# One decode step on a Trainium2 core: a load of sixteen rows of 64 bytes put ahead of the first weight load on SyncE's queue

## The chip, the cores and the metric

The kernel runs on one core of one Trainium2 chip. The metric is device time in microseconds (us) of one execution; lower is better. The kernel before was timed three times: 186.65, 186.67 and 186.84 us, median 186.67 us. Durations of single steps come from one more execution that the hardware profiler recorded. Its own time is 186.95 us, and its span, from the first to the last recorded instruction, is 185.7 us.

## The reference

One decode step of a transformer block for a batch of two tokens of width 640, all in bf16: attention over a cached window, then a gated feed-forward network, both modulated by a condition vector `c`.

```python
mod = (_silu(c) @ w_mod).reshape(2, 6, 1, 640)      # sa, ca, ga, sb, cb, gb
h = _layernorm(x) * (1 + ca) + sa
q = (h @ wq).reshape(B, Sq, 32, 192)                # 32 heads of 192
k, v = k_cache[:, :, Sk - W:], v_cache[:, :, Sk - W:]   # W = 1024 of 4096 rows
p = _softmax(einsum(q, k) * 192 ** -0.5)
x = x + ga * (einsum(p, v) @ wo)
h = _layernorm(x) * (1 + cb) + sb
x = x + gb * ((_gelu(h @ w_gate) * (h @ w_up)) @ w_down)
```

Every weight and every row of the cached window is used once, so each has to be brought in from HBM once: the page counts 76.88 MB read.

## The kernel before, in words

The big loads are all issued by SyncE (SP), one after the other, in the order in which the program lists them, through the helper at L252 (`e.dma_start`). All of them therefore show as "SPq L252" in the profile. That order is: `w_mod` (4800 KB, into place 1 of the tile `pp`), `A_wq` (7680 KB, into `r1`), four blocks of the k cache and four of the v cache (6144 KB each), `A_wo` in two pieces (5120 and 2560 KB), `B_w_gate` and `B_w_up` (1920 KB each), `B_w_down` in two pieces (1600 and 320 KB), and at the very end the store of the output (2.5 KB).

The first three loads (`w_mod`, `A_wq` and the first k block) wait for nothing. From the second k block on, each load first waits at L93 or L252 until the matrix multiplications that read the former content of its place are done, since the three places (two in `pp`, one in `r1`) are used in turn for the eight cache blocks, and the tail's weights reuse them too. The waits are written by the small scheduler `_Sched`: it keeps for each engine a list of operations in program order, and `emit` (L78 to L99) puts a semaphore wait in front of each operation for what it depends on.

ScalarE (ACT) issues the two small loads of `c` and `A_x` (eight rows of 320 bytes each) on its own queue. They are held back until GpSimd has cleared the tiles `cc` and `xc`.

The stages, in order:

- `silu(c)`, its transpose, and `mod0` and `mod1`: 40 products of `scT` with `w_mod` (L367). They wait for the load of `w_mod`.
- The first layer norm (L331 to L354) and its transpose into `hT` (L324).
- `q`: 60 products with `A_wq` (L388), a selection (L408) and the copy into `qbc` (L397).
- Scores: sixteen quarter-blocks of k. VectorE multiplies each by q in place (L432), TensorE sums it over the head dimension by products with an identity (L445, L418), VectorE reduces what is left (L452). Four further products without use (L425, L418) keep TensorE's clock up.
- Softmax (L458 to L479), then eight half-blocks of v: VectorE spreads the weights into `Em` (L483), TensorE multiplies (L498).
- `A_wo` (L577, 192 products), the second layer norm, gate and up (L593), gelu (L600), product (L604), transpose (L324), down (L613), the last two steps on VectorE (L619, L621), and the store.

The last thing that SP does is to wait until the output has landed (L626).

Of the kernel before, what the change touches and what calls it, by code (L numbers as in the profile page):

```python
# [8 lines left out]
BF16 = mybir.dt.bfloat16  # L9
# [94 lines left out]
def bass_adaLN_cond__sliding_block_cached__geglu_ffn__decode_kernel(  # L104
# [15 lines left out]
    P = 128  # L120
# [5 lines left out]
    SQ = 32  # L126
# [40 lines left out]
    with es:  # L167
        S = _Sched(nc, es)
        sb = lambda name, shape, dt: es.enter_context(nc.sbuf_tensor(name, shape, dt))
# [16 lines left out]
        oT = sb("oT", [P, NT, SQ], BF16)  # L186
        aC = sb("aC", [P, FN], BF16)
        aT = sb("aT", [P, FT, SQ], BF16)
        qbc = sb("qbc", [P, 2, Dh], BF16)
        ident_b = sb("ident_b", [P, P], BF16)  # L190
        ident_f = sb("ident_f", [P, P], F32)
# [46 lines left out]
            return ("bank", k)  # L238

        sem_x = S.sem("d_x")  # L240
        sem_c = S.sem("d_c")
        sem_wm = S.sem("d_wm")
        sem_wq = S.sem("d_wq")
# [7 lines left out]
        def k_dma(dst, src):  # L251
            return lambda e: e.dma_start(dst, src)  # L252
# [46 lines left out]
        def place_keys(k):  # L299
            return [("pl", k, q) for q in range(NH)]  # L300

        keep = {}
        S.dma("sp", k_dma(wm_f, w_mod.rearrange("(p k) n -> p (k n)", k=KT)), sem_wm, writes=place_keys(1), name="ld_wm")
        S.dma("sp", k_dma(wq_v.rearrange("p k n -> p (k n)"), A_wq.rearrange("(p k) n -> p (k n)", k=KT)),
              sem_wq, writes=place_keys(2) + ["wq"], name="ld_wq")
# [250 lines left out]
        for i, (ta, tb) in enumerate(wo_of):  # L556
# [5 lines left out]
              writes=["wg"], deps=dead, name="ld_wg")  # L562
        S.dma("sp", k_dma(wu_v.rearrange("p k n -> p (k n)"), B_w_up.rearrange("(p k) n -> p (k n)", k=KT)), sem_wu,
              writes=["wu"], deps=dead, name="ld_wu")
# [58 lines left out]
        S.dma("sp", k_dma(dram_rows(out[:, 0, :]), rows_of(sc)), sem_out, reads=["sc"], name="st_out")  # L623

        S.emit("sp", nc.sync)
        nc.sync.wait_ge(sem_out, 16)  # L626
        S.emit("act", nc.scalar)
        S.emit("pool", nc.gpsimd)
# [30 lines left out]
```

## Time and profile before

| | before |
|---|---|
| median of three timed runs | 186.67 us (186.65 to 186.84) |
| the profiled execution's own time | 186.95 us |
| its span | 185.7 us |
| busy: TensorE, VectorE, ScalarE, GpSimd | 110.3, 101.4, 13.1, 4.8 us |
| share of time of the 16 DMA engines on queue q1 (SP's and its big loads) | 96.4% |
| bytes read from HBM | 76.88 MB |
| issue of `w_mod`'s load to its landing | 14.2 us |

How to read it: the profiled execution is 0.28 us longer than the median of the timed runs, and 1.25 us of it lie around the span. Times inside the profile count from the start of the span. "SPq" rows are the time that SyncE's sequencer needs to issue one DMA; they are not the transfer. A transfer is cut into packets, one row of one partition each for these loads, and the 16 DMA engines work through their own packets independently. "us to landing" runs from the start of the issue until the last of the 16 engines has reported.

### The profile page before, as it was taken

The numbers are of one execution on the slowest core, as the hardware profiler recorded it, in microseconds if no ns is written. First come the engines' busy times: TensorE is split into PE (matmuls) and PEld (weight loads), VectorE is DVE, ScalarE is ACT, GpSimd is POOL, SyncE is SP. The second block draws the span as 40 slices with busy tenths as digits, with TensorE's granted clock in tenths as the row PEclk, the third lists the DMA queues.
The fourth block names the chain that finished last, engine by engine and source line by source line (L and its number), as shares of the span: only waits on it lengthen the run. The fifth ranks groups of instructions, "written<-read, shape, count | busy, mean of one in ns | idle before, by whom it ended". The sixth has DMA issues, their size and how long they took to land.

```text
span 185.7 us, 1833 instructions
## 1 busy us (share of the span) xinstructions
PE 110.3 (59%) x929; PEld 35.9 (19%) x699; DVE 101.4 (55%) x106; ACT 13.1 (7%) x22; POOL 4.8 (3%) x12
## 2 busy tenths in 40 slices
PE   0004500871089899988999885499464059095294
PEld 0001200340000000000000000366263036084121
DVE  6811500010588999999999994748479000301603
ACT  2002300023000000000000000200100000400310
POOL 8100000000000000000000000000000000000000
PEclk9999999998559999999999999569999558855558
DMA  7999998898999989898999989898999999899980
GB/s 256 406 464 490 424 490 384 349 491 371 487 434 413 489 360 487 371 487 381 466 438 413 487 360 487 381 476 381 459 455 402 468 424 418 366 432 424 423 368 24
DMA packets 2347, 76.99 MB, mean 415 GB/s; under 512 B 292, under 2 KB 292, under 8 KB 420
## 3 DMA queue, kind: packets, MB, share of 16 engines
q1 hardware_dynamic: 2316, 76.88, 96.4%
q8 instruction: 6, 0.10, 0.2%
q10 hardware_dynamic: 24, 0.01, 0.0%
q14 instruction: 1, 0.01, 0.0%
HBM read 76.88 MB, written 0.00 MB: 414 GB/s over the span
## 4 chain that ended last, share of the span: by engine, by line
DMA 45%; DVE 36%; PE 16%; issue 1%; SPq 1%; ACT 0%; DVEq 0%
DMA pp<-in_A_k_cache_dram 25%; DMA r<-in_A_wo_dram 19%; DVE pp L432 19%; DVE r L432 7%; PE ps L498 7%; DVE Sg L452 5%; PE ps L418 4%; PE ps L593 2%; PE ps L577 1%; DVE Em L483 1%; SPq L252 1%; PE ps L613 1%; PE ps L445 1%; DVE aT L324 0%; DVE M L458 0%
## 5 line engine op out<-in xcount | busy, mean ns | idle before, releaser
L432 DVE TENSOR_TENSOR pp<-pp,qbc 128x6144 bf16<-128x6144 bf16 x12 | 40.2, 3354 | 8.6 <-DMA pp<-in_A_k_cache_dram 8.6
L418 PE MATMUL ps<-pp,ident_b 128*128 128x512 bf16 x132 | 32.0, 393 | 0.0
L498 PE MATMUL ps<-pp,Em 128*64 128x384 bf16 x192 | 20.2, 379 | 14.2 <-DMA pp<-in_A_v_cache_dram 12.9
L483 DVE TENSOR_TENSOR Em<-E_sb,M32b 128x2048 bf16<-128x2048 bf16 x8 | 18.2, 2289 | 5.4 <-PE ps L498 4.7
L498 PEld LDWEIGHTS ps<-pp,Em 128*64 128x64 bf16 x192 | 13.9, 128 | 20.2 <-issue 9.5
L432 DVE TENSOR_TENSOR r<-r,qbc 128x6144 bf16<-128x6144 bf16 x4 | 13.4, 3356 | 0.0
L367 PE MATMUL ps<-pp,scT 128*32 128x480 bf16 x40 | 4.4, 601 | 15.1 <-DMA pp<-in_w_mod_dram 15.1
L452 DVE TENSOR_REDUCE Sg<-ps 128x32 f32<-128x512 f32 x16 | 11.0, 690 | 3.6 <-PE ps L418 3.6
L388 PE MATMUL ps<-r,hT 128*32 128x512 bf16 x60 | 6.0, 586 | 11.5 <-DMA r<-in_A_wq_dram 11.5
L418 PE MATMUL ps<-qbc,ident_b 128*128 128x384 bf16 x54 | 12.6, 346 | 0.0
L445 PE MATMUL ps<-pp,ident_b 128*128 128x512 bf16 x12 | 4.9, 407 | 12.8 <-DVE pp L432 12.8
L515 DVE TENSOR_SCALAR On<-ps,rden 32x192 bf16<-32x192 f32 x4 | 1.7, 417 | 17.0 <-PE ps L498 17.0
L418 PE MATMUL ps<-r,ident_b 128*128 128x512 bf16 x44 | 10.1, 379 | 0.0
L577 PE MATMUL ps<-r,oT 128*32 128x160 bf16 x192 | 6.8, 339 | 5.1 <-DMA r<-in_A_wo_dram 5.1
L399 DVE CAST qC<-ps 128x512 bf16<-128x512 f32 x1 | 0.7, 691 | 16.6 <-PE ps L388 16.6
L425 PEld LDWEIGHTS ps<-qbc,ident_b 128*128 128x128 bf16 x18 | 1.8, 98 | 38.4 <-issue 38.4
L577 PEld LDWEIGHTS ps<-r,oT 128*32 128x32 bf16 x192 | 6.1, 146 | 5.5 <-DMA r<-in_A_wo_dram 5.5
L425 PE MATMUL ps<-qbc,ident_b 128*128 128x384 bf16 x18 | 6.2, 345 | 0.7 <-ACT qbc L397 0.7
L582 DVE TENSOR_TENSOR lnt<-ps,modC 128x160 f32<-128x160 f32 x1 | 0.3, 324 | 11.2 <-PE ps L577 11.2
L472 ACT ACTIVATE E_sb<-Sg,nb 128x256 bf16<-128x256 f32 x2 | 1.0, 500 | 72.8 <-DVE nb L470 72.8
L445 PEld LDWEIGHTS ps<-pp,ident_b 128*128 128x128 bf16 x12 | 1.2, 97 | 23.4 <-DVE pp L432 22.8
L388 PEld LDWEIGHTS ps<-r,hT 128*32 128x32 bf16 x60 | 2.4, 140 | 15.4 <-issue 15.3
(76 smaller groups left out, 66.2 us busy)
## 6 DMA issues: line engine op xcount, KB each, us to landing
pp<-in_A_k_cache_dram SPq DMA_DIRECT2D x3, 6144.0 KB, 41.2
pp<-in_A_v_cache_dram SPq DMA_DIRECT2D x3, 6144.0 KB, 23.4
r<-in_A_wq_dram SPq DMA_DIRECT2D x1, 7680.0 KB, 31.9
r<-in_A_k_cache_dram SPq DMA_DIRECT2D x1, 6144.0 KB, 38.2
r<-in_A_v_cache_dram SPq DMA_DIRECT2D x1, 6144.0 KB, 23.0
r<-in_A_wo_dram SPq DMA_DIRECT2D x1, 5120.0 KB, 30.3
pp<-in_w_mod_dram SPq DMA_DIRECT2D x1, 4800.0 KB, 14.2
r<-in_A_wo_dram SPq DMA_DIRECT2D x1, 2560.0 KB, 36.0
```

The source lines that it names most:

```text
L252: return lambda e: e.dma_start(dst, src)
L367: last = e.matmul(ps[SQ * j:SQ * j + SQ, bk, 0:3 * DN].rearrange("p (i n) -> p i n", i=3), lhsT=scT[:, k, :], rhs=wm_v[:, k, 3 * part * D: ...
L388: last = e.matmul(ps[SQ * j:SQ * j + SQ, BK_H + c, 0:QW], lhsT=hT[:, k, :], rhs=wq_v[:, k, RN * j + QW * c:RN * j + QW * (c + 1)], start=( ...
L418: return e.add_instruction(i)
L425: last = put(ps[:, bk, 0:2 * Dh], lhsT=ident_b[:, :], rhs=qbc[:, :, :].rearrange("p b d -> p (b d)"), start=True, stop=True)
L432: S.op("dve", lambda e: e.tensor_tensor(out=places[k][:, JH * q:JH * (q + 1), :], in0=places[k][:, JH * q:JH * (q + 1), :], in1=qbc[:, b, ...
L445: last = put(o_ap, lhsT=ident_b[:, :], rhs=places[k][:, JH * q:JH * (q + 1), ci * GC:(ci + 1) * GC], start=(ci == 0), stop=(ci == NCH - 1))
L452: S.op("dve", lambda e: e.tensor_reduce(out=S_sb[:, b, a:a + JH], in_=ps[:, q % 2, 0:JH * GC].rearrange("p (j c) -> p j c", j=JH), axis=AX ...
L483: S.op("dve", lambda e: e.tensor_tensor(out=Em[:, t % 2, :, :], in0=E_sb[:, b, J * t:J * (t + 1)].unsqueeze(2).broadcast_to([P, J, H]), in ...
L498: last = e.matmul(ps[r:r + 2 * H, BK_O[b], 0:ON], lhsT=Em[:, t % 2, 2 * jp:2 * jp + 2, :].rearrange("p j c -> p (j c)"), rhs=places[k][:, ...
L577: last = e.matmul(ps[SQ * j:SQ * j + SQ, BK_M, 0:DN], lhsT=oT[:, t, :], rhs=wo_v[:, t, DN * j:DN * j + DN], start=(t == 0), stop=(t == NT ...
L593: last = e.matmul(ps[SQ * j:SQ * j + SQ, bk, 0:FN], lhsT=hT[:, k, :], rhs=wv[:, k, FN * j:FN * j + FN], start=(k == 0), stop=(k == KT - 1) ...
```

## The change

A new tile `first` of 128 partitions by 32 bf16 values (64 bytes a partition) is allocated between `aT` and `qbc`, which moves the tiles allocated after it by 64 bytes in each partition. SP gets a new DMA at the head of its list, ahead of the load of `w_mod`: it copies the first 64 bytes of each of the first sixteen rows of `w_mod` into partitions 0, 8, ..., 120 of `first`. It waits for nothing. Nothing reads `first`. Ahead of the wait for the output, SP waits for the semaphore of this load. What is computed is unchanged. On the other engines the instructions and their order are the same; on SP the one DMA is added in front and all others keep their order.

```diff
@@ -186,6 +186,7 @@
         aT = sb("aT", [P, FT, SQ], BF16)
+        first = sb("first", [P, SQ], BF16)
         qbc = sb("qbc", [P, 2, Dh], BF16)
@@ -238,6 +239,7 @@
         sem_x = S.sem("d_x")
+        sem_first = S.sem("d_first")
         sem_c = S.sem("d_c")
@@ -300,6 +302,7 @@
         keep = {}
+        S.dma("sp", k_dma(first[0:P:P // 16, :], w_mod[0:16, 0:SQ]), sem_first, writes=["first"], name="ld_first")
         S.dma("sp", k_dma(wm_f, w_mod.rearrange("(p k) n -> p (k n)", k=KT)), sem_wm, writes=place_keys(1), name="ld_wm")
@@ -623,6 +626,7 @@
         S.emit("sp", nc.sync)
+        nc.sync.wait_ge(sem_first, 16)
         nc.sync.wait_ge(sem_out, 16)
```

## The prediction, as put on record before the changed kernel ran

> **What bounds the kernel.** I read the page's DMA rows first. They say how full the transfer engines are.
>
> ```profile
> DMA  7999998898999989898999989898999999899980
> q1 hardware_dynamic: 2316, 76.88, 96.4%
> HBM read 76.88 MB, written 0.00 MB: 414 GB/s over the span
> ```
>
> The 40 slices are at 8 or 9 from the second to the next to last. Queue q1 alone fills 96.4% of 185.7 us, that is 179.0 us of every engine on the mean. TensorE with 59% and VectorE with 55% are far from that. So I ask whether the queue is ever empty in between. The list of DMA issues, cut to the moment of one issue, gives the time from issue to landing; these are the second half's loads, issued at 67.23, 82.70, 98.16 and 113.63 us:
>
> ```profile
> pp<-in_A_k_cache_dram SPq DMA_DIRECT2D x1, 6144.0 KB, 24.8
> pp<-in_A_v_cache_dram SPq DMA_DIRECT2D x1, 6144.0 KB, 23.9
> r<-in_A_v_cache_dram SPq DMA_DIRECT2D x1, 6144.0 KB, 23.0
> pp<-in_A_v_cache_dram SPq DMA_DIRECT2D x1, 6144.0 KB, 22.3
> ```
>
> They land at 92.0, 106.6, 121.2 and 135.9 us, 14.6 us apart. Each of the last three is issued 7.5 to 9.3 us before the one ahead of it has landed (113.63 against 121.2, for one). So each load stands in line behind its forerunner, and the compute that frees its place is early by at least 7.5 us. The chain of waits puts 36% of the span on VectorE, but that is the way to an issue that could have come later. Its last links show the true end:
>
> ```profile
> 132.29 0.34 SPq L252
> 132.63 0.05 issue
> 132.68 36.05 DMA r<-in_A_wo_dram
> 168.72 0.04 issue
> 168.77 2.35 PE ps L577 x53
> ```
>
> The second piece of `A_wo` lands at 168.72 us, 36 us after its issue, and from there plain compute runs to the end. The packet records of the trace confirm it: each of the 16 engines works from 1.81-2.58 us to 180-182 us with its packets end to end (a 38400-byte packet every 1.42 us). **The time is the start of the first packet, plus an unbroken stream to 168.72 us, plus about 17 us of tail.** Whatever moves the stream's head moves the end by as much.
>
> **The head.** SP's timeline:
>
> ```profile
> 0.79 0.39 SPq L252 DMA_DIRECT2D pp<-in_w_mod_dram  x1
> 1.24 0.41 SPq L252 DMA_DIRECT2D r<-in_A_wq_dram  x1
> ```
>
> Issues follow each other at 0.45 us (0.39 and 0.06 between). The DMA view of the first 4 us, in slices of 0.1 us, shows when packets start:
>
> ```profile
> GB/s 0 0 0 0 0 0 0 0 0 0 0 0 0 0 0 0 0 0 2688 1536 384 768 0 0 0 768 0 0 0 0 0 0 0 0 0 0 0 0 768 1920
> DMA packets 23, 0.88 MB, mean 221 GB/s; under 512 B 0, under 2 KB 0, under 8 KB 0
> ```
>
> A column of 384 is one packet. Sixteen start between 1.8 and 2.6 us (1.02 us after the issue began), and the next only from 3.8 us. By the packet records fifteen of these first ones take 1.79 to 2.46 us, one 1.43, where the later 112 of `w_mod` take 1.42; they end at 3.85 to 4.32 us, one at 4.71. So the head holds a ramp of 0.4 to 1.0 us per engine. This is where the change can lose or win.
>
> **The change, part by part.**
>
> 1. *The issue.* The new load is SP's first and starts at 0.79 us in `w_mod`'s place. No row shows an issue of 16 rows of 64 bytes. SP's own issues of two-dimensional loads take from 0.33 us (`B_w_gate`) to 0.44 (a `B_w_down` piece), one 0.87 right behind another one; the store of eight short rows takes 0.69. It cannot be below nothing, since SP issues in order. I take `w_mod`'s own row, also SP's first: 0.39, with the gap 0.45. Ends: 0.33 and 0.75. Every load behind it moves by this.
> 2. *The transfer.* 16 rows and 16 reports. The nearest rows are `c`'s and `A_x`'s packets of 320 bytes, 0.02 us each, and the 4-byte semaphore reports, 0.009 us. One of each per engine: 0.03 us on the stream. Ends 0 and 0.03.
> 3. *The ramp.* If `w_mod`'s packets have it as before, 0. If the small packet takes it in their place, `w_mod` starts at 1.81 + 0.48 = 2.29 and ends its first packets at 3.71 instead of 3.85 to 4.32: 0.14 to 0.61 us won net of the issue, 1.0 on the one late engine. I take 0. The ramp looks like the start of a large read: after an instruction packet of 16 KB on an engine, the next big packet is late too (2.37 us where 1.82 is usual, at 40.1 us), although that engine had been busy for 38 us and was anything but cold; while the 320-byte packets of `c`, also on another queue, cost the big packet after them nothing.
> 4. *The moved loads.* `A_wq`, the first k block and all after keep their order. Later issues wait for compute, which is 7.5 us early, so they stay in line. `w_mod` lands at about 15.5 instead of 15.0, `A_wq` and k move alike.
> 5. *ACT's small loads* start at 1.05 us as before, while SP issues. `c` is ready 4 us before `w_mod` lands (its silu runs at 9.95); cost 0. If this cover went, half a microsecond in `mod0` would still hide behind the 11.5 us that TensorE then waits for `A_wq`.
> 6. *The wait at the end* is for a load done some 180 us before, and stands while SP waits 1.0 us for the output anyway: 0. Nothing is queued behind it but that wait.
> 7. *The tiles moved by 64 bytes.* VectorE's rows for `qbc` and `Em` have 7.5 us of cover; in the tail, `Sg` and its neighbours are read by steps of 0.3 to 0.6 us each. No row shows an effect of an address; 0.
>
> **Sum.** 0.45 + 0.03 = 0.48 us. The profiled execution's 186.95 becomes 187.43. The timed runs lie 0.28 lower, so the median should go from 186.67 to **187.15 us** (+0.26%).
>
> The Trainium skill (page "DMA: Bandwidth & Descriptors", section "Anatomy of one DMA") puts a sequencer's dispatch at about 50 ns, for GpSimd's kind of DMA. By it the issue would cost 0.05, and the sum would be 0.08: 186.75. SP's measured rows of 0.33 to 0.87 us decide against it here.
>
> **The rivals.**
>
> - *The small load takes the ramp* (faster). First packets that follow another one run at 1.42 us at once. Place: the first packet of each engine. With the mean end of 4.10 going to 3.71, 0.39 us are won: 186.28; over the engines 186.06 to 186.53. It decides when more than 0.48 us of the ramp goes. For it: isolated 8 KB instruction packets ahead of the span take 0.36 to 0.53 us for what should take 0.30, so a first packet costs something even where nothing else is moving; two engines start 0.7 us late, which a first load would cover. Against it: point 3.
> - *Half of it* goes: about 0.35 us of the ramp against 0.48, 186.8, not to be told from no change.
> - *The issue costs the stream nearly nothing*: `w_mod`'s rows are ready when the small ones leave, and only the 0.06 gap and 0.03 of transfer remain: 186.76. Against it: packets start 1.02 us after the issue began, with no sign of idle engines waiting earlier.
> - *The two queues collide.* ACT issues `c` from 1.05 us and needs 1.11 us, against 0.54 for `A_x`; meanwhile SP's third issue takes 0.64 where its like takes 0.54. Now `w_mod`'s issue would be second and fall into that stretch, and could take 0.1 to 0.57 more: 187.25 to 187.7.
> - *The stream waits for the small load's report.* The store takes 0.69 + 1.0 us from issue to landing. If `w_mod` started only after as long, at 2.48 instead of 1.81, or another 1.02 after that, the price is 0.7 to 1.7: 187.3 to 188.4. Against it: 269 reports lie between packets in this trace and the next packet follows each without a gap. The same section of the skill fits a DMA's time as 2.0 us plus bytes by 436 GB/s; charged whole to this load it would give 188.7, and no pair of loads in this trace shows such a gap.
>
> That the change does not do what it says can only be the second and third rivals: the load is surely issued, first.
>
> **How the numbers follow.** About what a measurement of this kernel can tell from no change is 0.2%, 0.37 us. Full shift: 0.48, of which 0.05 lies within 0.37 us (issue at 0.33 or below). Ramp taken: 0.20, faster. Half: 0.17, same. Nearly free: 0.03, same. Collision 0.08 and waiting for the report 0.04, slower. Faster 0.20, same 0.05 + 0.17 + 0.03 = 0.25, slower 0.43 + 0.12 = 0.55. The range goes from 186.1 (the ramp won on nearly every engine) to 187.5 (the dearest issue, 0.75 + 0.03, gives 187.45); beyond it lie most of the collision and the report, and the best of the first rival, together about 0.15. The forecast's own range is 187.0 to 187.45.
>
> **What would show it.** In the profile after: SP's second row, `w_mod`'s issue, at about 1.24 us; first 38400-byte packets at about 2.3 us that again take some 2 us; `w_mod` landing near 15.5, `A_wo`'s second piece near 169.2, and the tail from there unchanged at 17 us. If the first big packets take 1.42 us, the first rival is right. The forecast is wrong if those packets end before 4.3 us on the engines that land last, if the tail changes its length, or if a code packet of 16 KB falls on another engine (each costs that engine about 1.5 us: 0.9 to 1.1 itself and 0.5 on the next packet).

## The result and the profile after

The changed kernel takes 187.67 us (median of 6 runs, 187.47 to 187.78), the kernel before 186.84 us (6 runs beside them, 186.65 to 187.00). The ratio is 1.0044, 95% interval 1.0034 to 1.0055: 0.83 us slower, where 0.48 was forecast, and 0.17 us beyond the upper end of the range, 187.5. (Beside these runs the kernel before itself took 0.17 us more than the 186.67 from which the forecast started; the difference of 0.83 is still more than the +0.78 of the dearest issue that the range allowed for.) The profiled execution took 187.62 us (before: 186.95), its span is 186.4 us (185.7).

The page's DMA rows are as full as they were; the first of the 40 slices fell from 7 to 4, and the last ones show no rest that could have taken the loss up.

```profile
DMA  4999999999989899999989999998999999999990
...
q1 hardware_dynamic: 2348, 76.88, 96.1%
...
HBM read 76.88 MB, written 0.00 MB: 413 GB/s over the span
```

SP's timeline after (start, duration, what):

```profile
0.79 0.62 SPq L254 DMA_DIRECT2D first<-in_w_mod_dram  x1
1.47 0.57 SPq L254 DMA_DIRECT2D pp<-in_w_mod_dram  x1
2.09 0.42 SPq L254 DMA_DIRECT2D r<-in_A_wq_dram  x1
2.55 0.62 SPq L254 DMA_DIRECT2D pp<-in_A_k_cache_dram  x1
```

The last row, the issue of the first k block, starts at 1.69 us in the kernel before:

```profile
1.69 0.64 SPq L252 DMA_DIRECT2D pp<-in_A_k_cache_dram  x1
```

The added load's issue takes 0.62 us, not 0.39, and the issue of `w_mod` 0.57 instead of 0.39. `w_mod`'s issue starts at 1.47 where 1.24 was expected. By the first k block SP is 0.86 us late. The DMA view of the first 4 us, again in slices of 0.1 us:

```profile
GB/s 0 0 0 0 0 0 0 0 0 0 0 0 0 0 0 0 0 0 0 0 0 3 3 3 13 13 768 1920 1920 384 768 0 0 0 0 384 0 0 0 0
DMA packets 60, 0.62 MB, mean 155 GB/s; under 512 B 44, under 2 KB 44, under 8 KB 44
```

The columns of 3 at 2.1 to 2.4 us are the small packets (the last of the sixteen falls into the next column); those of 13 are `c`'s packets, which now come before `w_mod`'s. The big ones (384 is one) start at 2.65 us, before at 1.81: 0.85 us later. By the packet records their sixteen first ones take 1.65 to 2.56 us and end at 4.95 us on the mean, before at 4.11: 0.84 later. The ramp of the first big packets is all there.

From here the stream carries the shift unchanged. Mean ends of the engines, by the packet records: `A_wq` 32.17 before and 33.00 after (+0.83), `A_wo`'s second piece 167.27 and 168.16 (+0.89). The loads are in line as before; from issue to landing:

```profile
pp<-in_A_k_cache_dram SPq DMA_DIRECT2D x1, 6144.0 KB, 24.8
...
pp<-in_A_v_cache_dram SPq DMA_DIRECT2D x1, 6144.0 KB, 23.8
...
r<-in_A_v_cache_dram SPq DMA_DIRECT2D x1, 6144.0 KB, 22.9
...
pp<-in_A_v_cache_dram SPq DMA_DIRECT2D x1, 6144.0 KB, 22.0
```

These are within 0.3 us of those before: each is issued 1.30 us later (68.53 us against 67.23 for the first of them), and each of the last three still 7.4 to 9.3 us before the one ahead of it has landed, so they stand in line as before. The end of the chain differs:

```profile
143.30 39.41 DMA pp<-in_B_w_down_dram
182.70 0.14 issue
182.84 1.04 PE ps L616 x48
183.88 0.02 issue
183.90 0.34 DVE lnt L622
184.24 0.02 issue
184.26 0.32 DVE sc L624
```

The chain no longer comes by way of `A_wo` and the layer norm; it comes straight from the large piece of `B_w_down`, which lands at 182.70 us (143.30 + 39.41); the small one follows by the semaphore records at 183.45 us, while the products run. So two things end together in the tail, the stream itself and the compute behind `A_wo`, and both hang on the head of the stream. Which of them comes last differs from run to run: the chain goes by way of `A_wo` in e2 and e12, which have the load in front, and by way of `B_w_down` in e1, which does not.

### The profile page after: what moved, and what is told of

Its sections match the earlier page's. It is cut to its first block, busy times and chain, and to the rows that moved or that the text cites. A ratio compares the mean times of both kernels' runs of the same rounds, so it can differ in the third digit from the quotient of the medians.

```text
span 186.4 us, 1834 instructions
## 1 busy us (share of the span) xinstructions
PE 108.5 (58%) x929; PEld 35.1 (19%) x699; DVE 101.3 (54%) x106; ACT 13.1 (7%) x22; POOL 4.8 (3%) x12
## 4 chain that ended last, share of the span: by engine, by line
DMA 58%; DVE 31%; PE 7%; SPq 1%; issue 0%; DVEq 0%
DMA pp<-in_A_k_cache_dram 25%; DMA pp<-in_B_w_down_dram 21%; DVE pp L435 19%; DMA pp<-in_A_v_cache_dram 12%; DVE r L435 7%; DVE Sg L455 5%; PE ps L421 3%; PE ps L501 3%; SPq L254 1%; PE ps L616 1%; PE ps L448 1%; DVE lnt L622 0%; DVE sc L624 0%; DVEq L93 0%; SPq L93 0%
## 5 line engine op out<-in xcount | busy, mean ns | idle before, releaser
L421 PE MATMUL ps<-qbc,ident_b 128*128 128x384 bf16 x54 | 12.1, 333 | 0.0
L580 PE MATMUL ps<-r,oT 128*32 128x160 bf16 x192 | 5.9, 310 | 5.7 <-DMA r<-in_A_wo_dram 5.7
L580 PEld LDWEIGHTS ps<-r,oT 128*32 128x32 bf16 x192 | 5.4, 134 | 6.1 <-DMA r<-in_A_wo_dram 6.1
L428 PE MATMUL ps<-qbc,ident_b 128*128 128x384 bf16 x18 | 6.1, 336 | 0.7 <-ACT qbc L400 0.7
```

The costliest lines, as they stand in the source:

```text
L421: return e.add_instruction(i)
L428: last = put(ps[:, bk, 0:2 * Dh], lhsT=ident_b[:, :], rhs=qbc[:, :, :].rearrange("p b d -> p (b d)"), start=True, stop=True)
L580: last = e.matmul(ps[SQ * j:SQ * j + SQ, BK_M, 0:DN], lhsT=oT[:, t, :], rhs=wo_v[:, t, DN * j:DN * j + DN], start=(t == 0), stop=(t == NT ...
```

## The experiments

The theory to be tested, formed from the profile after: the whole loss is made in the first 2.7 us on SP's queue, 0.68 us by the added issue with its gap (0.62 + 0.06) and 0.17 by the slower start of `w_mod` behind it (issue to first packet 1.18 us instead of 1.02). Against it: the shifted addresses, the transfer and its report, the collision of SP's and ACT's issues, and later a finer question, what of the head really costs. All runs stand beside runs of the kernel before on the same chip.

**e1, the tile without the load.**

```diff
-        S.dma("sp", k_dma(first[0:P:P // 16, :], w_mod[0:16, 0:SQ]), sem_first, writes=["first"], name="ld_first")
-        nc.sync.wait_ge(sem_first, 16)
```

> The tile of 64 bytes and its semaphore stay, the load and its wait are left out. Issue theory (the whole +0.83 us is SP's time to issue the added load, 0.68, and a slower issue of w_mod behind it, 0.17): time as before, ratio 0.999 to 1.001, first big packet at 1.81 us. Address theory (tiles moved by 64 bytes are slower to read or write): +0.3 us or more with the head as before.

Measured: 186.76 us against 186.73, ratio 1.0002 (0.9993 to 1.0010). The addresses cost nothing that can be measured.

**e2 and e3, ACT's small loads held back**, with the change (e2) and without it (e3).

```diff
-        S.dma("act", ... sem_c, writes=["cc"], name="ld_c")
-        S.dma("act", ... sem_x, writes=["xc"], name="ld_x")
...
-        S.op("pool", lambda e: e.memset(oT[:, :, :], 0.0), ...)
+        held_by = S.op("pool", lambda e: e.memset(oT[:, :, :], 0.0), ...)
+        S.dma("act", ... sem_c, writes=["cc"], deps=[held_by], name="ld_c")
+        S.dma("act", ... sem_x, writes=["xc"], deps=[held_by], name="ld_x")
```

> The changed kernel, with ACT's two small loads held back until GpSimd's last clearing ends (5.6 us), so that SP issues alone. Issue theory with collision: the added load's issue falls from 0.62 to 0.40-0.55 and w_mod's from 0.57 to 0.39; first big packet at about 2.3 to 2.4 us; +0.45 to +0.6 us over before. Without collision (the two issues cost by their own shape and order): the rows stay at 0.62 and 0.57, first big packet at 2.65, +0.8 us as without the hold.

> The kernel before with the same hold, to take the hold's own effect off the run with both. Expected by every theory: w_mod's issue 0.39 at 0.79 us, first big packet at 1.8 us, within 0.1 us of before, since c lands later but still ahead of w_mod (15.0 us) or at most 1 us behind it, under TensorE's 11.5 us of waiting for A_wq. A loss over 0.2 us would say that the hold itself costs.

Measured: e2 187.69 us against 186.73, ratio 1.0048 (1.0036 to 1.0060); e3 186.69, ratio 0.9998 (0.9989 to 1.0006). SP's timeline of e2, and under it ACT's:

```profile
0.80 0.63 SPq L254 DMA_DIRECT2D first<-in_w_mod_dram  x1
1.48 0.57 SPq L254 DMA_DIRECT2D pp<-in_w_mod_dram  x1
2.10 0.42 SPq L254 DMA_DIRECT2D r<-in_A_wq_dram  x1
```

```profile
5.61 1.10 ACTq L254 DMA_DIRECT2D cc<-in_c_dram  x1
6.74 0.54 ACTq L254 DMA_DIRECT2D xc<-in_A_x_dram  x1
```

SP issues alone, and its rows stay as they were. `c`'s own issue takes 1.10 us alone too, so the 1.11 that the prediction read as a sign of two queues in each other's way was none. The collision has fallen.

**e4, the same load issued by ACT**, ahead of `c`.

```diff
-        S.dma("sp", k_dma(first[0:P:P // 16, :], w_mod[0:16, 0:SQ]), ..., name="ld_first")
+        S.dma("act", k_dma(first[0:P:P // 16, :], w_mod[0:16, 0:SQ]), ..., name="ld_first")
```

> The same sixteen rows of 64 bytes, issued by ACT ahead of c instead of by SP. Issue theory: SP's head is free again, first big packet at about 1.8 to 1.9 us, time within 0.2 us of before (a collision of the two queues could leave w_mod's issue at up to 0.57, then +0.2). Transfer theory (the small packets or their reports on the engines delay the big ones, whoever issues them): +0.5 us or more again.

Measured: 186.73 us against 186.73, ratio 0.9998 (0.9989 to 1.0006); ACT needs 0.61 us for the issue, SP's rows and the first big packet (1.82 us) are those of before. So the same load costs nothing when another queue brings it. Its packets then come at 5.15 to 5.89 us, behind the first big ones; so this run does not show what small packets ahead of the big ones cost the engines themselves.

**e6, the same load on SP, behind the first three.**

```diff
         load_next()
+        S.dma("sp", k_dma(first[0:P:P // 16, :], w_mod[0:16, 0:SQ]), sem_first, writes=["first"], name="ld_first")
```

> The same load, but issued by SP behind w_mod, A_wq and the first k block. Issue theory: SP then waits anyway until 21.8 us for its fifth load, so the issue hides; first big packet at 1.8 us; ratio 0.999 to 1.001. If the load costs the stream by its transfer or by its report, wherever it stands: +0.3 us or more.

Measured: 186.72 us against 186.80, ratio 0.9996 (0.9988 to 1.0004). The issue takes 0.59 us at 2.38 us and nobody waits for it. Its packets come at 46.3 to 48.0 us, in line behind the first k block. e4 and e6 together leave only the place: ahead of the stream, on its queue.

**e7, two such loads in front.**

```diff
+        S.dma("sp", k_dma(second[0:P:P // 16, :], w_mod[16:32, 0:SQ]), sem_second, writes=["second"], name="ld_second")
```

> Two such loads in front (rows 0 to 15 and 16 to 31 of w_mod, into two tiles). Issue theory: the second costs one more issue with its gap, 0.45 to 0.68 us, so the first big packet starts at 3.1 to 3.35 us and the time is +1.3 to +1.55 us over before. If only the first DMA of a queue is dear (a cost of starting, paid once), the second costs 0.2 us or less: +0.9 to +1.1.

Measured: 188.24 us against 186.80, +1.44 us, ratio 1.0081 (1.0064 to 1.0099). The issues take 0.63, 0.57 and, for `w_mod`, 0.58 us; the big packets start at 3.31 us, 1.51 later than before. SP's issue of the first k block starts at 3.20 us, also 1.51 later. Each load pays; nothing is paid once for all.

**e5, the same rows from one contiguous kilobyte.**

```diff
-        S.dma("sp", k_dma(first[0:P:P // 16, :], w_mod[0:16, 0:SQ]), ...
+        S.dma("sp", k_dma(first[0:P:P // 16, :], w_mod[0, 0:16 * SQ].rearrange("(r n) -> r n", r=16)), ...
```

> The added load reads 1024 bytes in one piece (the first 512 values of w_mod's row 0) as sixteen rows of 64 bytes, instead of the heads of sixteen rows; the destination is the same. Form theory (SP needs longer to issue a copy whose source steps): the added load's issue falls from 0.62 to 0.33-0.44 us, w_mod's to about 0.42, first big packet at 2.25 to 2.35, +0.45 to +0.55 us over before. Order theory (0.62 for any short load that SP issues first, 0.57 for what follows it): rows as in the changed kernel, first big packet at 2.65, +0.8 to +0.95 us.

Measured: 187.61 us against 186.80, ratio 1.0041 (1.0028 to 1.0054); rows of 0.63 and 0.57 us, first big packet at 2.67. The stepping source is not what makes the issue long.

**e8, 128 rows of 64 bytes; e10, sixteen rows into adjacent partitions; e12, 64 rows into adjacent partitions.**

```diff
-        S.dma("sp", k_dma(first[0:P:P // 16, :], w_mod[0:16, 0:SQ]), ...
+        S.dma("sp", k_dma(first[:, :], w_mod[0:P, 0:SQ]), ...          # e8
+        S.dma("sp", k_dma(first[0:16, :], w_mod[0:16, 0:SQ]), ...      # e10
+        S.dma("sp", k_dma(first[0:64, :], w_mod[0:64, 0:SQ]), ...      # e12
```

> 128 rows of 64 bytes in front instead of 16, one per partition. If the issue goes by the form alone and not by the rows: issue 0.62, w_mod's 0.57, first big packet at 2.65 to 2.7, +0.8 to +0.95 us, as with 16 rows. If it goes by the number of rows: an issue of 0.9 us or more, and +1.1 us or more.

> Sixteen rows of 64 bytes into sixteen adjacent partitions (0 to 15) instead of every eighth. Step theory (the 0.62 us of the added load's issue, against 0.39 with 128 rows, come from stepping over partitions): issue 0.39, small packets from 1.8 us. Count theory (they come from having sixteen rows): issue 0.62 and small packets from 2.18 us again. The time: +0.65 to +0.9 us over before by both, since with 128 rows the big packets also started 0.73 us late.

> 64 rows of 64 bytes into 64 adjacent partitions. If only loads over all 128 partitions are issued in 0.39 us: 0.55 to 0.65 here, small packets from about 2.18. If the count matters in steps of rows per engine (one row each is slow, several are not): 0.39 and 1.8. The time +0.6 to +0.9 us over before by both.

Measured, each against the kernel before beside it: e8 1.0040 (1.0025 to 1.0054), +0.80 us; e10 1.0042 (1.0028 to 1.0055), +0.81 us; e12 1.0048 (1.0034 to 1.0062), +0.90 us. SP's timeline of e10, and the DMA view of its first 4 us:

```profile
0.80 0.40 SPq L254 DMA_DIRECT2D first<-in_w_mod_dram  x1
1.26 0.40 SPq L254 DMA_DIRECT2D pp<-in_w_mod_dram  x1
1.70 0.69 SPq L254 DMA_DIRECT2D r<-in_A_wq_dram  x1
2.43 20.68 SPq L254 DMA_DIRECT2D pp<-in_A_k_cache_dram  x2
```

```profile
GB/s 0 0 0 0 0 0 0 0 0 0 0 0 0 0 0 0 0 1 5 4 0 0 0 0 10 1539 1542 1158 1152 0 384 0 384 0 0 0 0 0 0 0
DMA packets 60, 0.62 MB, mean 155 GB/s; under 512 B 44, under 2 KB 44, under 8 KB 44
```

This is the run that says most. SP's first two rows are, to 0.02 us, those on which the forecast was built: 0.40 each, `w_mod` issued at 1.26. The small packets start at 1.80 us, as the big ones did before. And yet the big ones start only at 2.54 us, 0.75 after them, and the time is +0.81. e8 shows the same (0.39 and 0.41, small packets from 1.79, big ones at 2.53). In e12 the issue takes 0.59 and the small packets start at 2.14, but the big ones at 2.64. So the length of the added load's issue row is not what the head costs. Whatever that row says, 0.73 to 0.86 us pass from the old start of the stream to the new one. (The 0.39 of e8 was expected by neither reading; the 0.40 of e10 fits the step theory, and the 0.59 of e12, without any step, says that stepping is not the whole reason.)

The missing time does stand among SP's rows, but further on: in e8 and e10 the third issue, `A_wq`'s, takes 0.69 us, where it takes 0.41 in the kernel before and 0.42 in the changed one. SP therefore comes late to the next issue, that of the first k block (the last row above joins it with the one after it). The delay of that issue against 1.69 us, and the delay of the first big packet against 1.81 us, are 0.74 and 0.73 us in e8, 0.74 and 0.74 in e10, 0.83 and 0.83 in e12, 0.86 and 0.85 in the changed kernel, 1.51 and 1.51 in e7. Which of the two holds up the other, or whether one thing holds up both, these runs do not show.

**e11 and e13, a load in front that carries something.** Nothing is added; `w_mod`'s own load is cut in two by columns.

```diff
-        S.dma("sp", k_dma(wm_f, w_mod.rearrange("(p k) n -> p (k n)", k=KT)), sem_wm, ...
+        S.dma("sp", k_dma(wm_f[:, 0:1920], w_mod.rearrange("(p k) n -> p (k n)", k=KT)[:, 0:1920]), sem_first, writes=["wm_head"], ...
+        S.dma("sp", k_dma(wm_f[:, 1920:], w_mod.rearrange("(p k) n -> p (k n)", k=KT)[:, 1920:]), sem_wm, ...
...
-             S.op("pe", f, reads=["scT"] + place_keys(1), ...
+             S.op("pe", f, reads=["scT", "wm_head"] + place_keys(1), ...
# e13: 640 in place of 1920
```

> No added load; instead w_mod's own load is cut in two, ahead 3840 bytes of each of the 128 rows (0.49 MB), behind it the other 34560 bytes, so SP issues one DMA more in front of everything else just as in the changed kernel. Preparation theory (a DMA needs about 0.7 us to be made ready behind the one ahead of it, which costs only when the one ahead leaves the engines idle that long): the head's packets start at 1.8 us and keep the engines busy for 1.14 us and the ramp, the rest follows without a gap, ratio 0.999 to 1.0015. Issue theory as I had it (each issue ahead of the bulk shifts the stream, whatever it carries): +0.45 to +0.85 us.

> As with the head of 3840 bytes a row, but a head of 1280 bytes a row: 0.16 MB, 0.38 us of the stream at 432 GB/s, against the 0.73 us by which the big packets came late behind 64-byte rows. Preparation theory, loss = 0.73 us less what the load ahead keeps the engines busy: if that is 0.38 us, +0.3 to +0.4 us over before, with the packets of the second piece from 2.5 us and the engines idle for some 0.3 us in front of them; if the head's packets also carry the ramp of 0.4 to 1.0 us that every first big packet shows, the engines stay busy past 2.5 us and the loss is under 0.15 us. If any short load in front costs the full shift: +0.75 us.

Measured: e11 186.66 us against 186.69, ratio 0.9996 (0.9987 to 1.0005). One DMA more is issued ahead of the bulk, and nothing is lost. The DMA view of its first 4 us shows why:

```profile
DMA  0000000000000000009699459276979989999999
GB/s 0 0 0 0 0 0 0 0 0 0 0 0 0 0 0 0 0 0 269 77 154 154 115 115 269 115 269 269 538 307 384 499 346 730 999 925 1123 1389 733 691
```

The head's packets fill the engines from 1.8 to 3.3-4.0 us, and by the packet records most first packets of the second piece then take 1.28 us, their usual time: the ramp had been paid in the head. In e8 and the changed kernel the columns between the small and the big packets are empty or nearly so.

e13 measured 187.59 us against 186.77, ratio 1.0045 (1.0030 to 1.0060): +0.82, where I had given +0.3 to 0.4 by one reading and under 0.15 by the other. Its trace shows a smaller loss in the stream than the clock does: `A_wq`'s mean end is 0.50 us later than in the kernel before, `A_wo`'s second piece 0.52. The head's packets run from 1.82 to 2.73 us, and the first packets of the second piece, from 2.69 us, show the ramp again (1.38 to 2.27 us, 1.37 usual). The second piece starts 0.88 us after the old start of the stream (2.69 against 1.81), and 0.38 us of its work had been done by then: that leaves the 0.50 of the stream. The profiled execution lost 0.63; its twelve runs spread from 186.91 to 188.87 us, and the interval of the ratio reaches down to +0.56, so how much lies between the stream and the clock stays open. The reading that the ramp would hide it was wrong; the plain one, any short load costs the full shift, fits the time (+0.75 given) but not the stream.

## Why the prediction was wrong

*What bounds the kernel: right.* A shift at the head comes out at the end nearly one to one: +0.85 at the first big packet, +0.83 in the time; with two loads +1.51 and +1.44; with e10 +0.74 and +0.81; with none at the head (e1, e3, e4, e6) or none lost there (e11) no change. Only e13, with 0.50 in the stream and +0.82 in the time, falls out.

*Step 1, the issue: this is the step that failed.* "`w_mod`'s own row, also SP's first: 0.39, with the gap 0.45", and every load behind moves by this. First, the row was not 0.39 but 0.62, inside the ends given. Second, and that is the error in kind, the added load's row and its gap are not the whole price: the prediction let every load behind it move by this one row and left the issue of `w_mod` as it was. The price runs to the first packet of the next load, and that came later after the start of its issue: 1.02 us in the kernel before, behind the small load 1.18 (changed kernel), 1.28 (e8 and e10) and 1.21 (e7). In the changed kernel the sum is 0.45 as forecast, 0.23 for the longer row of the added load and 0.18 for `w_mod`'s own row (0.57 instead of 0.39), together 0.86 against the measured 0.85. In e10 both rows came out as forecast and the shift was 0.74 all the same. Behind packets that keep the engines busy this costs nothing (e6, e11); at the head the engines stand idle for it.

*Step 2, the transfer: nothing speaks against it*, but it was not tested apart. The small packets take 0.008 us each, and the load costs nothing inside the stream (e4, e6); whether its packets or reports hold an engine up at the head is part of what stays open.

*Step 3, the ramp: right.* Sixteen small packets took nothing off it: mean end minus first start of the sixteen first big packets is 2.30 us before and 2.29 after. What takes most of it is a head that keeps all engines at work for longer (e11), at no gain.

*Steps 4 to 7: right* within the measurement: the order held, ACT's loads came earlier (the silu at 4.08 us instead of 9.95), the addresses cost nothing (e1), and neither does the wait at the end, which e4 and e6 keep.

*The rivals.* The first (ramp taken), half of it, and the nearly free issue did not happen. The collision had the right size for the time (187.25 to 187.7) and the wrong cause: e2 shows the same rows with SP alone. The report comes nearest, since 0.7 and more was its price; but by the semaphore records the last report of the small load lands at 2.70 us in the changed kernel and at 2.76 in e12, after the first big packets (2.65 and 2.64), and in e10 it lands at 2.31, 0.23 us before them. So the next load does not wait for the whole report. That each engine waits for its own report is not excluded where the reports come late (in the changed kernel the first of them lands at 2.48 us); in e10, where all have landed 0.23 us before, something else is waited for. And within the stream, as the prediction said, the packets follow the reports of a load without a gap.

*The range* ended at 0.75 + 0.03 because I bounded the price by the row of the added load alone, and among the rows that I had I left out the longest: the 0.87 us of an issue right behind another one, which step 1 names, and which with its gap would have reached past +0.85. That the next load's issue might grow I had only in the collision, with a cause that e2 took away.

*The tail*: the prediction expected it unchanged at 17 us; after `A_wo`'s landing it is 0.3 us shorter in the profile. The twenty products with `B_w_up` ran in 1.00 us where they had taken 1.79, at a granted clock of 0.97 of full speed against 0.50. Most of that gains nothing, because the products with `B_w_down` then wait for its large piece, which lands at 182.70 us. It is not the change that brings it: in e2 and e12, also with the load in front, the same products take 1.79 us.

What stays open: why the issue takes 0.59 to 0.63 us for sixteen rows into every eighth partition and for 64 adjacent rows, but 0.39 to 0.40 for sixteen adjacent and for 128; and what is being done in the 0.48 to 0.75 us between the small packets and the next load's first one. Issued by ACT at the same time, or by SP later, the load costs nothing (e4, e6); whether the time that it costs in front passes in SP's queue or on the engines is not shown.

The Trainium skill (page "DMA: Bandwidth & Descriptors", section "Anatomy of one DMA", for GpSimd's kind of DMA) calls generating the descriptors small and says that the fixed cost is dominated by completion and not by setup. Here, on SP's queue, a small load ahead costs the next one 0.73 us or more when the engines have nothing else to do (e8, e10). How much of that is setup no run here shows; that it is not the whole of the small load's completion, the changed kernel and e12 show.

## What to carry to other kernels

Where the profile shows the DMA engines full from the first packet to the last, the first microseconds of the queue are on the critical path: put the largest load first there and everything small behind it or on another queue, where it cost nothing here (e4, e6). Its own data then come later: they landed at 7.66 us in e4 and only behind the first k block in e6, at 2.70 in the changed kernel. A short load in front did not warm anything for the big one; it cost the time until the next load's first packet, which was longer than its own issue row showed. Price a step at the head of a queue by when the next one's packets start; part of the price can stand in the issue rows of the loads behind it.

## What the runs showed of the hardware that was not expected

- On SP's queue `w_mod` shows its first packet 1.02 us after its issue begins when it is the first load, and 1.18 to 1.28 us behind a short load. Short loads that are themselves the first show theirs after 0.99 and 1.00 us (e8, e10, issue rows of 0.39 and 0.40) to 1.39 (changed kernel, 0.62).
- In the kernel before, the changed kernel, e7, e8, e10 and e12 the first big packet starts 0.10 to 0.12 us after SP begins the issue of the first k block, however many loads stand in front and however long their rows are.
- The first issue of eight rows of 320 bytes on ACT takes 1.05 to 1.13 us and the next of the same shape 0.54 or 0.55, whether SP issues at the time or not, and also with another small load ahead of it (e4).
- The first packets of a big load are slow (1.65 to 2.56 us for what later takes 1.42) also when each engine has just moved a 64-byte packet; with 3840-byte rows in front (30 KB an engine) most are not (1.28 us, the usual time there), with 1280-byte rows (10 KB an engine) they are again.
